# One core, attention + FFN + 2-D FFT + FFN: two groups of rows moved behind the second weight matrix, squares to a free tile, a third staging tile for part of the first matrix

## The chip, the core and the metric

One NeuronCore of one Trainium2 chip runs the whole program in one launch. The metric is device time in microseconds (us) of one execution, and the time of a kernel is the median of its runs.

## What is computed

Inputs are q, k, v of 4 batches x 8 heads x 576 positions x 64, two feed-forward networks (FFNs) and a layer-norm gain; everything is float32.

```python
# attention, block-causal with blocks of 64
scores = scale * q @ k.T
scores = where(i // 64 >= j // 64, scores, -1e9)
attn   = softmax(scores) @ v                 # heads side by side: x is 4 x 576 x 512
# FFN 1
xn = (x - mean) / sqrt(var + 1e-6) * g_ln
x  = x + relu(xn @ w_ch1) @ w_ch2            # 512 -> 2048 -> 512
# FFT mixing and FFN 2
u  = x + real(fft(fft(x, axis=1), axis=2))
un = (u - mean) / sqrt(var + 1e-6)
out = u + relu(un @ w2_ch1) @ w2_ch2
```

## The kernel before

TensorE works in f16 here. A float32 operand is split into a high and a low f16 half, and each product is the sum of three f16 matmuls (high x high, high x low, low x high).

**Rows.** The 576 rows of each batch are split in three. E is the first 256 rows, F the next 256, and the last 64 rows of all four batches together form L (256 rows). So there are nine column blocks for each FFN: E0 to E3, F0 to F3 and L. FFN 1 goes over them in the order E0 E1 E2 E3 F0 F1 L F2 F3.

**Attention for E** (`e_items`): 16 units, one for a batch and a pair of heads. A unit loads q, k and v, makes fp32 scores (TensorE, L716), takes maxima (VectorE, L730, L731), the exponential (ScalarE, L734), splits the result into halves (ScalarE L688, VectorE L689), has it transposed by a DMA that SP issues (L695), multiplies it with v (TensorE, `pv`, L664; v is split by L677) and normalises (VectorE, L702, L705, L768).

**Attention for F and L** (`attention_items`): 16 units of three steps. Scores are L876, and the results leave through L943 (into `N`) and by GpSimd's DMAs (L970) into `XxF` and `XxL`. These units need another set of buffers, which is opened by `a_switch`. That item needs the whole second weight matrix of FFN 1 (`("W", 1, 2, 3)`) and the last rows of E (`("X1", "E3")`).

**Weights of FFN 1.** The two matrices have four chunks (`c`) each, and each chunk comes in two pieces of 1 MB: 16 pieces. `piece(k)` first lets SP load piece k + PL, with PL = 1 (`w_load`, L179, into a tile of the tag `stage`, of which there are ST = 2). Then come `w_raw` (ScalarE, L191) and `w_decode`: ScalarE writes a shifted copy into the one tile `sign` (L204), VectorE puts the bits together (L208, L211), and after two operations of VectorE ScalarE squares the chunk so far (L221), to get the sum of squares for the scale. The squares themselves are not used, and they are written over the raw piece in the stage tile. When the two pieces of a chunk of the first matrix are decoded, `w_hi` (ScalarE, L288) and `w_lo` (VectorE, L296) write the two halves into a tile `wq`. Chunks of the second matrix wait for scales that take all of them into account, made by `w_balance` (L249 to L259) after the last piece.

**FFN 1.** `gemm1` (L515, 192 matmuls of 128x256 for a column block), relu and split (ScalarE L524, VectorE L525), then `gemm2` (L540, 96 matmuls of 128x512) or, for E0, E1 and F3, `gemm2_both` (L570); its output is added by L555. Ahead of it stands the layer norm (L433 to L482), whose result is transposed by a DMA on SP (L483). L's tiles are `bn1L`, `ln1L`, `xs` and `xnT1L`.

**Order.** No engine order is written out. The items above stand in streams; `merge` takes the next item from the stream with the smallest virtual time, if what the item needs has been issued. Every engine then works through its own instructions in that program order. Tiles of one tag go round in a pool (`w` has 9, each 16 KB a partition), and the first write to a tile waits for the last reader of what was there.

**After FFN 1's attention** `a_end` frees the attention's buffers, and `w_second` loads and decodes the weights of FFN 2 with the same functions (32 pieces of 512 KB, two staging tiles of the tag `wr`); then come the DFT's matmuls and FFN 2.

Of the kernel before, what the change touches and what calls it, by code (L numbers as in the profile page):

```python
# [10 lines left out]
I32 = mybir.dt.int32  # L11
BF16 = mybir.dt.bfloat16
# [23 lines left out]
LNP = ()  # L36
NZ = (1, 2)
PL = 1
S_W0 = 0.0
E1B = (3, 2, 2)  # L40
NB = 1
# [20 lines left out]
S_E2 = 50.0  # L62
# [21 lines left out]
def fused_kernel(ctx: ExitStack, tc: tile.TileContext, io: dict):  # L84
# [4 lines left out]
    wpool = ctx.enter_context(tc.tile_pool(name="wpool", bufs=1))  # L89
# [61 lines left out]
    def all_sum(src, n, name):  # L151
        r = sm.tile([128, n], F32, tag="ar", name=name)
        nc.gpsimd.partition_all_reduce(r, src, 128, bass_isa.ReduceOp.add)
        return r


    W = {}
    wst = {"n": 0, "loaded": []}

    def w_stage(n, name):  # L160
        shape = [128, n, 512, 2]
        if "pool" in wst:
            return wst["pool"].tile(shape, I32, tag="wr", bufs=WR, name=name)
        return a_tile(shape, I32, "stage", name)

    def w_signs(pool, n, bufs):
# [29 lines left out]
    def w_decode(ffn, which, c, i, n):  # L196

        r = W.pop(("raw", ffn, which, c, i))
        dst = W["st", ffn, which, c][:, i:i + n, :]
        di = dst.bitcast(I32)  # L200
        hw, lw = r[:, :, :, 1], r[:, :, :, 0]
        z = wst["z"][wst["n"] % len(wst["z"])]
        wst["n"] += 1
        nc.scalar.activation(  # L204
            out=z[:, :, :, 1], in_=hw.bitcast(F32), func=AF.Copy, scale=float(2.0 ** -100)
        )
        zi = z.rearrange("p n f w -> p n (f w)").bitcast(I32)
        nc.vector.scalar_tensor_tensor(  # L208
            out=di, in0=di, scalar=3, in1=zi, op0=ALU.logical_shift_left, op1=ALU.bitwise_or
        )  # L210
        nc.vector.scalar_tensor_tensor(  # L211
            out=di, in0=lw, scalar=29, in1=di, op0=ALU.logical_shift_right, op1=ALU.bitwise_or
        )
        m = SQ[ffn - 1]
        if i == 0:
            W["n2", ffn, which, c] = sm.tile([128, 4 // m], F32, tag="wn", bufs=3, name="wn")
        if (i + n) % m:
            return
        rb = r.rearrange("p n f w -> p (n f w)").bitcast(BF16)
        k = i + n - m  # L220
        nc.scalar.activation(  # L221
            out=rb[:, 0:512 * m].rearrange("p (n f) -> p n f", n=m),
            in_=W["st", ffn, which, c][:, k:k + m, :], func=AF.Square,
            accum_out=W["n2", ffn, which, c][:, k // m:k // m + 1],
        )

    def w_total(ffn, which, c):

        n2 = W.pop(("n2", ffn, which, c))
        if n2.shape[-1] > 1:  # L230
            n1 = sm.tile([128, 1], F32, tag="wn1", bufs=2, name="wn1")
            nc.vector.tensor_reduce(out=n1, in_=n2, axis=AX.X, op=ALU.add)
            n2 = n1
        W["tot", ffn, which, c] = all_sum(n2, 1, "wt")
        if which == 1:
            W["t", ffn, which, c] = w_tile(ffn, which, c)

    def w_scale(ffn, which, c):
# [33 lines left out]
    def w_tile(ffn, which, c):  # L272
        if ffn == 2 and which == 1:
            return wst["pool"].tile([128, 2, 2048], F16, tag="w", bufs=2, name=f"wq{ffn}{which}{c}")
        return wpool.tile([128, 2, 2048], F16, tag="w", bufs=9, name=f"wq{ffn}{which}{c}")
# [92 lines left out]
    def w_items():  # L368

        n = WN[0]  # L370
        pieces = [(which, c, i) for which in (1, 2) for c in range(4) for i in range(0, 4, n)]

        def load(k):
            if k < len(pieces):
                w_load(1, *pieces[k], n)

        todo = []

        def piece(k):
            which, c, i = pieces[k]  # L380
            load(k + PL)
            w_raw(1, which, c, i, n)
            w_decode(1, which, c, i, n)
            scales()
            if i + n == 4:
                w_total(1, which, c)
                todo.append((which, c))

        def scales():

            for which, c in todo:
                w_scale(1, which, c)
                if which == 1:
                    w_hi(1, which, c)
                    w_lo(1, which, c)
            todo.clear()

        def end(c):
            if c == 0:
                scales()  # L400
                w_balance(1)
            w_hi(1, 2, c)
            w_lo(1, 2, c)

        first = [(0.0, lambda k=k: load(k), (), None) for k in range(PL)]
        out = ([], [])
        for k, (which, c, i) in enumerate(pieces):
            gives = ("W", 1, 1, c - 1) if which == 1 and i == 0 and c > 0 else None
            out[which - 1].append((float(n), lambda k=k: piece(k), (), gives))
        out[0].append((0.0, scales, (), ("W", 1, 1, 3)))  # L410
        for c in range(4):
            out[1].append((1.0, lambda c=c: end(c), (), ("W", 1, 2, c)))
        return first, out[0], out[1]
# [190 lines left out]
    def a_tile(shape, dt, tag, name):  # L604
        return ap_["p"].tile(shape, dt, tag=tag, bufs=ap_["b"][tag], name=name)
# [167 lines left out]
    def e_items(b):  # L773
        def head():
            e_raw(b, 0)
            e_load(b)

        def front(p):
            if p + 1 < NPAIR:
                e_raw(b, p + 1)  # L780
            e_s(b, p)
            e_exp(b, p)
            e_norm_p(b, p)

        def back(p):
            e_pv(b, p)
            e_x(b, p)

        out = [(0.0, head, (), None), (3.0, lambda: front(0), (), None), (1.0, lambda: e_v(b), (), None)]
        for p in range(1, NPAIR):  # L790
            out.append((3.0, lambda p=p: (front(p), back(p - EL) if p >= EL else None), (), None))
        for p in range(NPAIR - EL, NPAIR):
            out.append((1.0, lambda p=p: back(p), (), ("X1", ("E", b)) if p == NPAIR - 1 else None))
        return out
# [440 lines left out]
    if True:  # L1235
# [31 lines left out]
        a_open(dict(stage=ST, rv=RVE, raw=RAWE, vh=2, vl=2, e=E1B[0], P=E1B[1], PT=E1B[2], xnT0=1, xn0=X0B, xs0=X0B))  # L1267
        w_signs(ap_["p"], WN[0], NZ[0])
        AE = [e_items(b) for b in range(B)]
        A1 = [(0.0, a_switch, (("W", 1, 2, 3), ("X1", ("E", 3))), None)]  # L1270
        A1 += attention_items([(b, p) for b in range(B) for p in range(NPAIR)])
        A1 += [(0.0, a_end, (), ("X1", "L"))]

# [67 lines left out]
        for c in range(4):  # L1341
# [6 lines left out]
            (0.0, 1.0, LN),  # L1348
            (0.0, 1.0, AE[0]),
            (S_E1, 1.0, AE[1]),  # L1350
            (S_E2, 1.0, AE[2] + AE[3]),
            (S_W0, 1.0, WF),
            (S_W1, R_W, WA),
            (S_W2, R_W, [(0.0, lambda: None, (("W", 1, 1, 3),), None)] + WB1),
            (S_F, 1.0, FF),
            (S_A1, R_A1, A1),
            (S_D, R_D, D),
# [104 lines left out]
```

## Time and profile before

| | |
|---|---|
| median of 3 runs | 1038.68 us (1035.98 to 1040.9) |
| the profiled execution | 1037.72 us, of which the span in the trace is 1035.9 us |
| busy: TensorE (PE) | 941.0 us, 91% of the span |
| busy: VectorE (DVE), ScalarE (ACT), GpSimd (POOL) | 617.5, 501.7, 83.9 us |
| mean granted TensorE clock | 0.959 of full speed (full speed is 2.4 GHz, the other level 1.2 GHz) |

A row of a timeline gives the start in us from the span's start, the duration in us, the engine, the line and operation, out<-in and a count; square brackets tell how long the engine was idle before and what released it. SPq is the DMA queue that SP issues on, and its rows are the time of issuing, not of moving.

### The profile page before, as it was taken

Reading aid. Unit: us, or ns where it says so; the run is one execution under the profiler, and the core shown is the slowest. Engines: PE = TensorE matmul, PEld = TensorE weight load, DVE = VectorE, ACT = ScalarE, POOL = GpSimd, SP = SyncE. Lnnn points to the kernel's source line nnn. Section 1 sums busy time; section 2 is a strip of 40 time slices with the busy share of each in tenths; the row PEclk is TensorE's granted clock in tenths of the full one; section 3 lists DMA queues with packets and bytes.
Section 4 is the critical chain, followed back from the end, with each engine's and each line's share of the span. In section 5 each row is a group of like instructions: output and inputs, shape, how many; then the busy total and the mean of one; then the engine's idle time right before and its main releaser. Section 6 shows DMA issues by size and latency. Waiting matters only on the chain.

```text
span 1035.9 us, 18326 instructions
## 1 busy us (share of the span) xinstructions
PE 941.0 (91%) x7226; PEld 645.6 (62%) x7226; DVE 617.5 (60%) x1501; ACT 501.7 (48%) x884; POOL 83.9 (8%) x217
## 2 busy tenths in 40 slices
PE   5467859889899989999998979999999999999998
PEld 4355644467476566576574756767668577586673
DVE  5879788777777876675477979865332332222120
ACT  6678775667677677535466765632111021120110
POOL 2101001000202002031011111100000000000000
PEclk9578978999999999999999989999999999999999
DMA  7876865456767758446415275630110100200100
GB/s 204 227 169 187 228 155 111 92 117 139 152 147 135 148 118 161 86 117 174 102 41 148 86 222 194 218 87 12 31 31 11 41 21 22 31 22 31 31 11 21
DMA packets 172439, 110.84 MB, mean 107 GB/s; under 512 B 146893, under 2 KB 155094, under 8 KB 170816
## 3 DMA queue, kind: packets, MB, share of 16 engines
q1 hardware_dynamic: 170032, 105.41, 41.4%
q0 software_dynamic: 2320, 4.25, 1.8%
q8 instruction: 57, 0.93, 0.4%
q14 instruction: 30, 0.25, 0.1%
HBM read 59.95 MB, written 11.01 MB: 68 GB/s over the span
## 4 chain that ended last, share of the span: by engine, by line
PE 45%; DVE 5%; DMA 4%; ACT 2%; issue 1%; POOL 0%; ACTq 0%; DVEq 0%
PE g L515 20%; PE g L540 19%; PE g L570 4%; DMA wr<-in_w 3%; DMA xnT1L<-xs 1%; PE ya L1143 1%; ACT wr L221 1%; DVE ws L211 1%; PE pq L1174 1%; DVE ws L208 1%; DVE hT L525 1%; ACT sign L204 1%; DVE wq L296 1%; PE pq L1164 1%; PE pf L1164 1%
## 5 line engine op out<-in xcount | busy, mean ns | idle before, releaser
L515 PEld LDWEIGHTS <-wq 128*128 128x128 f16 x3456 | 338.0, 99 | 66.9 <-ACT wq L288 6.2
L540 PE MATMUL g<-wq,hT 128*128 128x512 f16 x1440 | 331.2, 379 | 0.6 <-DVE XxE L555 0.6
L540 PEld LDWEIGHTS <-hT 128*128 128x128 f16 x1440 | 139.9, 98 | 161.1 <-issue 4.4
L524 ACT ACTIVATE hT<-g 128x512 f16<-128x512 f32 x144 | 84.5, 590 | 241.5 <-PE g L515 241.4
L525 DVE SCALAR_TENSOR_TENSOR hT<-g,hT 128x512 f16<-128x512 f32 x144 | 98.6, 687 | 140.6 <-ACT hT L524 140.4
L664 PE MATMUL pv<-vh,PT 128*128 128x65 f16 (+1 forms) x800 | 106.8, 206 | 32.9 <-DMA PT<-P 26.6
L664 PEld LDWEIGHTS <-PT 128*128 128x128 f16 x1200 | 85.0, 102 | 61.0 <-DMA PT<-P 29.4
L876 PE MATMUL st<-k,qz 128*128 128x512 f16 (+2 forms) x288 | 80.9, 334 | 13.8 <-ACT e L898 13.8
L689 DVE SCALAR_TENSOR_TENSOR P<-e,P 128x768 f16<-128x768 f32 (+2 forms) x64 | 62.0, 971 | 40.3 <-ACT P L688 39.9
L898 ACT ACTIVATE e<-st,aq,acf 128x384 f32<-128x384 f32 (+2 forms) x80 | 56.8, 740 | 53.7 <-DVE aq L893 48.9
L664 PE MATMUL pv<-vl,PT 128*128 128x64 f16 (+1 forms) x400 | 66.9, 205 | 3.0 <-DVE vl L677 3.0
L570 PE MATMUL g<-wq,hT 128*128 128x512 f16 x288 | 66.2, 388 | 0.7 <-DVE wq L296 0.7
L191 ACT ACTIVATE ws<-wr 128x512 f32<-128x512 f32 (+1 forms) x48 | 39.5, 827 | 43.4 <-DMA wr<-in_w 40.9
L688 ACT ACTIVATE P<-e 128x768 f16<-128x768 f32 (+2 forms) x64 | 54.4, 858 | 3.8 <-DMA PT<-P 2.3
L208 DVE SCALAR_TENSOR_TENSOR ws<-ws,sign 128x512 int32<-128x512 int32 (+1 forms) x48 | 41.5, 866 | 19.7 <-ACT sign L204 18.0
L716 PE MATMUL st<-raw 128*128 128x128 f32 (+1 forms) x128 | 39.5, 449 | 15.1 <-ACT e L734 7.6
L482 DVE TENSOR_TENSOR xs<-xn,xs 128x512 f16<-128x512 f32 x36 | 24.6, 687 | 45.4 <-ACT xs L476 45.4
L570 PEld LDWEIGHTS <-hT 128*128 128x128 f16 x288 | 28.7, 100 | 35.6 <-issue 3.8
L476 ACT ACTIVATE xs<-xn 128x512 f16<-128x512 f32 x36 | 22.4, 625 | 57.9 <-DMA xnT2('E', 3)_10326<-xs 7.8
L204 ACT ACTIVATE sign<-wr 128x512 f16<-128x512 f32 (+1 forms) x48 | 46.5, 968 | 5.7 <-DMA wr<-in_w 4.3
L892 DVE TENSOR_REDUCE aq<-st 128x2 f32<-128x768 f32 (+2 forms) x48 | 46.6, 972 | 2.5 <-PE st L684 1.7
L221 ACT ACTIVATE wr<-ws 128x512 bf16<-128x512 f32 (+1 forms) x40 | 35.3, 882 | 25.8 <-DVE ws L211 22.7
(385 smaller groups left out, 1298.8 us busy)
## 6 DMA issues: line engine op xcount, KB each, us to landing
wr<-in_w SPq DMA_DIRECT2D x16, 1024.0 KB, 5.9
wr<-in_w SPq DMA_DIRECT2D x32, 512.0 KB, 4.1
rawv<-in_vt SPq DMA_DIRECT2D x16, 320.0 KB, 3.8
rawqk<-in_kt SPq DMA_DIRECT2D x16, 288.0 KB, 2.9
out<-out SPq DMA_DIRECT2D x18, 256.0 KB, 2.0
d<-ws SPq DMA_DIRECT2D x4, 1024.0 KB, 5.0
ws<-d SPq DMA_DIRECT2D x4, 1024.0 KB, 7.9
rawqk<-in_qt SPq DMA_DIRECT2D x32, 80.0 KB, 3.4
```

Of the source, the lines that this page charges most:

```text
L204: nc.scalar.activation(out=z[:, :, :, 1], in_=hw.bitcast(F32), func=AF.Copy, scale=float(2.0 ** -100))
L208: nc.vector.scalar_tensor_tensor(out=di, in0=di, scalar=3, in1=zi, op0=ALU.logical_shift_left, op1=ALU.bitwise_or)
L515: nc.tensor.matmul(out=ps[:, i, :], lhsT=w1(ffn, k, wh, m), rhs=xt[:, xh, k, :], start=(n == 0), stop=(n == 3 * KT - 1),)
L524: nc.scalar.activation(out=h[:, :, 0, :], in_=ps, func=AF.Relu)
L525: nc.vector.scalar_tensor_tensor(out=h[:, :, 1, :], in0=ps, scalar=0.0, in1=h[:, :, 0, :], op0=ALU.max, op1=ALU.subtract,)
L540: nc.tensor.matmul(out=ps, lhsT=h[f // 4][:, f % 4, hh, t * 128:(t + 1) * 128], rhs=w2(ffn, f, wh), start=(f == 0 and hh == 0 and wh == 0) ...
L570: nc.tensor.matmul(out=g2["b"][t], lhsT=h[f // 4][:, f % 4, hh, t * 128:(t + 1) * 128], rhs=w2(ffn, f, wh), start=(f == 0 and hh == 0 and ...
L664: nc.tensor.matmul(out=out[..., 0:w], lhsT=l, rhs=v[..., 0:w], start=(n == 0), stop=(n == len(mm) - 1))
L688: nc.scalar.activation(out=P[:, 0, 0:n], in_=e, func=AF.Copy, scale=PSC)
L689: nc.vector.scalar_tensor_tensor(out=P[:, 1, 0:n], in0=e, scalar=PSC, in1=P[:, 0, 0:n], op0=ALU.mult, op1=ALU.subtract)
L876: nc.tensor.matmul(out=st[:, h, 0:n] if j < 4 else sf[:, o:o + n], lhsT=qz[:, a, q:q + 128], rhs=k[:, c, o:o + n], start=(i == 0), stop=(j ...
L898: nc.scalar.activation(out=e[:, h], in_=st[:, h], func=AF.Exp, scale=cf, bias=nb[:, h:h + 1],)
```

## The change

Line numbers of the changed kernel are higher than those of before by 4 (loads, L179 is L183), 15 (FFN and attention, L515 is L530, L876 is L891) and so on.

1. The stream of E2 and E3's attention gets an empty first item that needs chunk 0 of the second matrix to be issued in its final form. E2 and E3 therefore follow that chunk in program order, where they ran beside the weights before.
2. The squares of FFN 1's weights go into a tile of the tag `w`: for the first matrix into the tile that receives `wq` afterwards, for the second matrix into one tile for all chunks. The stage tile has its last reader at the second operation of VectorE (L211, now L215) instead of the square. FFN 2's squares stay in place.
3. Pieces 2, 5 and 8 are staged in a tile of the tag `w` in place of a stage tile, and up to piece 10 the load runs two pieces ahead, behind that one.

```diff
--- before.py
+++ after.py
@@ -36,6 +36,7 @@
 LNP = ()
 NZ = (1, 2)
 PL = 1
+T3 = 10
 S_W0 = 0.0
 E1B = (3, 2, 2)
 NB = 1
@@ -161,6 +162,9 @@
         shape = [128, n, 512, 2]
         if "pool" in wst:
             return wst["pool"].tile(shape, I32, tag="wr", bufs=WR, name=name)
+        wst["k"] = wst.get("k", -1) + 1
+        if wst["k"] % 3 == 2 and wst["k"] < T3:
+            return wpool.tile(shape, I32, tag="w", bufs=9, name=name)
         return a_tile(shape, I32, "stage", name)
 
     def w_signs(pool, n, bufs):
@@ -216,8 +220,16 @@
             W["n2", ffn, which, c] = sm.tile([128, 4 // m], F32, tag="wn", bufs=3, name="wn")
         if (i + n) % m:
             return
-        rb = r.rearrange("p n f w -> p (n f w)").bitcast(BF16)
         k = i + n - m
+        if ffn == 1:
+
+            if which == 1 or c == 0:
+                W["sq"] = w_tile(1, which, c)
+            if which == 1:
+                W["t", 1, which, c] = W["sq"]
+            rb = W["sq"][:, 0, :].bitcast(BF16)
+        else:
+            rb = r.rearrange("p n f w -> p (n f w)").bitcast(BF16)
         nc.scalar.activation(
             out=rb[:, 0:512 * m].rearrange("p (n f) -> p n f", n=m),
             in_=W["st", ffn, which, c][:, k:k + m, :], func=AF.Square,
@@ -232,7 +244,7 @@
             nc.vector.tensor_reduce(out=n1, in_=n2, axis=AX.X, op=ALU.add)
             n2 = n1
         W["tot", ffn, which, c] = all_sum(n2, 1, "wt")
-        if which == 1:
+        if (ffn, which) == (2, 1):
             W["t", ffn, which, c] = w_tile(ffn, which, c)
 
     def w_scale(ffn, which, c):
@@ -375,10 +387,13 @@
                 w_load(1, *pieces[k], n)
 
         todo = []
+        state = {"next": PL}
 
         def piece(k):
             which, c, i = pieces[k]
-            load(k + PL)
+            while state["next"] <= (k + 2 if k + 2 <= T3 else k + 1):
+                load(state["next"])
+                state["next"] += 1
             w_raw(1, which, c, i, n)
             w_decode(1, which, c, i, n)
             scales()
@@ -1267,6 +1282,7 @@
         a_open(dict(stage=ST, rv=RVE, raw=RAWE, vh=2, vl=2, e=E1B[0], P=E1B[1], PT=E1B[2], xnT0=1, xn0=X0B, xs0=X0B))
         w_signs(ap_["p"], WN[0], NZ[0])
         AE = [e_items(b) for b in range(B)]
+        AE2 = [(0.0, lambda: None, (("W", 1, 2, 0),), None)] + AE[2]
         A1 = [(0.0, a_switch, (("W", 1, 2, 3), ("X1", ("E", 3))), None)]
         A1 += attention_items([(b, p) for b in range(B) for p in range(NPAIR)])
         A1 += [(0.0, a_end, (), ("X1", "L"))]
@@ -1348,7 +1364,7 @@
             (0.0, 1.0, LN),
             (0.0, 1.0, AE[0]),
             (S_E1, 1.0, AE[1]),
-            (S_E2, 1.0, AE[2] + AE[3]),
+            (S_E2, 1.0, AE2 + AE[3]),
             (S_W0, 1.0, WF),
             (S_W1, R_W, WA),
             (S_W2, R_W, [(0.0, lambda: None, (("W", 1, 1, 3),), None)] + WB1),
```

**TensorE at the first score of F and L** (`st<-k`, from line L876 to L891). `g` is an FFN's PSUM output; `hT` is the activation of FFN 1. Before:

```order
L570 LDWEIGHTS hT
L570 MATMUL g_1690<-wq_1766,hT 128x512
L876 LDWEIGHTS qz_1798
L876 MATMUL st<-k_1837,qz_1798 128x384
L570 LDWEIGHTS hT
```

Now:

```order
L530 LDWEIGHTS wq_378
L530 MATMUL g_2077<-xnT1('E', 2)_1995,wq_378 128x256
L891 LDWEIGHTS qz_1910
L891 MATMUL st<-k_1938,qz_1910 128x384
L530 LDWEIGHTS wq_378
```

Before, 384 matmuls of `gemm1` (E0 and E1) and 91 matmuls of `gemm2_both` stand ahead of the first score; now all 192 of `gemm2_both` for E0 and E1 stand ahead of it, and 4 of E2's `gemm1` too, while 10 of the 16 units of E, not 16, are transposed ahead of the last load of weights. At the other end, 30 matmuls of `gemm1` and 96 of `gemm2` stand between the last `pv` and L's first matmul before, and 32 of `gemm2` now.

**VectorE at the end of the attention** (`rr` is the reciprocal that follows a `pv`, `bn1L` the first step of L's layer norm). Before:

```order
L943 TENSOR_TENSOR N_5101<-pv,rr 128x128
L525 SCALAR_TENSOR_TENSOR hT<-g_5705,hT 128x2x256
L525 SCALAR_TENSOR_TENSOR hT<-g_5762,hT 128x2x256
L433 BN_STATS bn1L_6032<-XxL 128x6
L434 BN_AGGR ln1L<-bn1L_6032 128x2
L433 BN_STATS bn1L_6035<-XxL 128x6
L433 BN_STATS bn1('F', 2)0_6419<-XxF_5224 128x6
L434 BN_AGGR ln1L<-bn1L_6035 128x2
L525 SCALAR_TENSOR_TENSOR hT<-g_5789,hT 128x2x256
L702 TENSOR_SCALAR rr<-pv,pw 128x2
```

Now:

```order
L717 TENSOR_SCALAR rr<-pv,pw 128x2
L720 RECIPROCAL rr<-rr 128x2
L448 BN_STATS bn1L_6033<-XxL 128x6
L449 BN_AGGR ln1L<-bn1L_6033 128x2
L448 BN_STATS bn1L_6036<-XxL 128x6
L448 BN_STATS bn1('F', 2)0_6471<-XxF_5403 128x6
L449 BN_AGGR ln1L<-bn1L_6036 128x2
L449 BN_AGGR ln1('F', 2)_6470<-bn1('F', 2)0_6471 128x2
L451 TENSOR_SCALAR ln1L<-ln1L 128x2
L448 BN_STATS bn1('F', 2)1_6474<-XxF_5403 128x6
L454 TENSOR_SCALAR ln1L<-ln1L 128x2
L570 SCALAR_TENSOR_TENSOR XxF_4446<-g_5893,winv_1266,XxF_4446 128x512
```

L's layer norm stood ahead of the last `rr` (the last rows of before), and now it stands behind it; an output of `gemm2` of F1 (L570, which was L555) now stands inside its chain.

**SP at the same place** (`wr_...<-in_w_2` are the first loads of FFN 2's weights). Before:

```order
L695 DMA_TRANSPOSE PT<-P 128x16x128
L695 DMA_TRANSPOSE PT<-P 128x10x128
L483 DMA_TRANSPOSE xnT1L<-xs 128x8x128
L179 DMA wr_6293<-in_w_2 128x1024
L179 DMA wr_6342<-in_w_2 128x1024
L483 DMA_TRANSPOSE xnT1L<-xs 128x8x128
```

Now:

```order
L710 DMA_TRANSPOSE PT<-P 128x16x128
L710 DMA_TRANSPOSE PT<-P 128x10x128
L183 DMA wr_6156<-in_w_2 128x1024
L183 DMA wr_6193<-in_w_2 128x1024
L498 DMA_TRANSPOSE xnT1L<-xs 128x8x128
L183 DMA wr_6255<-in_w_2 128x1024
L183 DMA wr_6289<-in_w_2 128x1024
L498 DMA_TRANSPOSE xnT1L<-xs 128x8x128
```

Two loads of FFN 2's weights moved ahead of the first transpose of L's rows, and two more ahead of the second.

## Rows read from the trace of the kernel before

**Rows 1.** The page: span, and DMA issues (KB each, us to landing).
```profile
span 1035.9 us, 18326 instructions
...
wr<-in_w SPq DMA_DIRECT2D x16, 1024.0 KB, 5.9
```

**Rows 2.** Windows: length, then PE, PEld, DVE, ACT, POOL busy, clock, DMA share, GB/s.
```profile
25.00:157.00 132.00, 87.00 (x759) 71.22 (x757) 108.09 (x268) 99.58 (x151) 12.04 (x33) 0.76 0.78 194
...
188.00:458.00 270.00, 249.07 (x2375) 170.31 (x2373) 200.60 (x521) 184.65 (x336) 28.14 (x74) 0.99 0.63 129
...
524.00:700.00 176.00, 166.16 (x1177) 117.03 (x1175) 148.56 (x370) 109.19 (x210) 22.78 (x59) 0.97 0.47 146
700.00:1036.00 336.00, 332.12 (x2292) 223.97 (x2289) 89.25 (x179) 46.61 (x78) 0.20 (x2) 1.00 0.09 24
```

**Rows 3.** ScalarE's groups, 0 to 260 us: busy, mean ns | idle before, releaser.
```profile
L204 ACT ACTIVATE sign<-wr 128x1024 f16<-128x1024 f32 x16 | 21.8, 1361 | 1.3 <-DVE ws L208 1.3
L191 ACT ACTIVATE ws<-wr 128x1024 f32<-128x1024 f32 x16 | 18.2, 1140 | 20.8 <-DMA wr<-in_w 20.8
...
L221 ACT ACTIVATE wr<-ws 128x2048 bf16<-128x2048 f32 x8 | 15.3, 1910 | 4.8 <-DVE ws L211 4.8
```

**Rows 4.** A wait of SP's queue, 0 to 260 us: us in total, times, longest.
```profile
SPq L179 <- ACT wr L221: 19.8, 4, 6.6
```

**Rows 5.** VectorE's groups, 0 to 260 us: busy, mean ns | idle before.
```profile
L689 DVE SCALAR_TENSOR_TENSOR P<-e,P 128x768 f16<-128x768 f32 x21 | 20.0, 952 | 6.4 <-ACT P L688 6.1
...
L730 DVE TENSOR_REDUCE eq<-st 128x2 f32<-128x512 f32 x16 | 10.9, 681 | 0.0
...
L768 DVE TENSOR_TENSOR XxE<-pv,rr 128x256 f32<-128x256 f32 x16 | 6.7, 420 | 0.0
L730 DVE TENSOR_REDUCE eq<-st 128x2 f32<-128x256 f32 x16 | 6.7, 419 | 9.4 <-PE st L684 9.4
...
L677 DVE SCALAR_TENSOR_TENSOR vl<-rv,pw,vh 128x1024 f16<-128x1024 f32 x4 | 5.1, 1280 | 1.4 <-ACT vh L676 1.4
...
L705 DVE RECIPROCAL rr<-rr 128x4 f32<-128x4 f32 x16 | 2.8, 173 | 0.1
```

**Rows 6.** Timelines at the balance: VectorE, then TensorE up to the first score.
```profile
156.92 0.22 DVE L259 TENSOR_SCALAR wsc<-wz,wzm 128x4 f32<-128x4 f32 x1
160.31 20.09 PE L570 MATMUL g<-wq,hT 128*128 128x512 f16 x89 [0.65 <-DVE wq L296]
180.24 0.33 PE L876 MATMUL st<-k,qz 128*128 128x384 f16 x1
```

**Rows 7.** TensorE's timeline: scores of a unit of E, and a start after idling.
```profile
81.60 1.11 PE L716 MATMUL st<-raw 128*128 128x256 f32 x4
...
88.81 8.04 PE L515 MATMUL g<-xnT,wq 128*128 128x256 f16 x50 [6.04 <-DVE ln1('E', 1)_787 L451]
```

**Rows 8.** TensorE's timeline from the last `pv` to L.
```profile
455.83 0.22 PE L664 MATMUL pv<-vh,PT 128*128 128x130 f16 x1
455.89 3.44 PE L515 MATMUL g<-xnT1('F', 1)_5363,wq 128*128 128x256 f16 x30
459.17 20.88 PE L540 MATMUL g<-wq,hT 128*128 128x512 f16 x96
479.89 13.30 PE L515 MATMUL g<-xnT1L,wq 128*128 128x256 f16 x120
```

**Rows 9.** L's layer norm: GpSimd's and VectorE's timelines, then the chain that ended last.
```profile
449.43 1.00 POOL L970 DMA_DIRECT2D XxL<-N  x2
451.40 0.69 DVE L433 BATCH_NORM_STATS2 bn1L<-XxL 128x6 f32<-128x512 f32 x1
458.22 2.29 DMA XxF<-N
464.08 10.03 DMA xnT1L<-xs
```

**Rows 10.** SP's timeline while the stage tiles are full.
```profile
24.36 7.30 SPq L695 DMA_TRANSPOSE PT<-P  x2
```

## The prediction

> **What bounds the kernel now.** I read the windows first, because the span is made of stages with different limits. From 700 us on, TensorE is busy for 332.1 of 336 us, and from 524 to 700 for 166.2 of 176 [rows 2]: behind L the end moves with TensorE's work, and only some 10 us of gaps can be won there. From 188 to 458 us it is busy for 249.1 of 270, so 21 us of gaps. From 25 to 157 us it is busy for 87 of 132, at a mean clock of 0.76, while VectorE is busy for 108.1 and ScalarE for 99.6 [rows 2]. This is the stage in which weights are decoded and E's attention runs, and neither engine is full: 23.9 us of VectorE's time there is idle, 18%.
>
> Next I asked what ends the idle time. ScalarE's first operation on a piece (L191) stood idle for 20.8 us, all of it for the weights' DMA [rows 3]. SP's own wait for a free stage tile is 19.8 us in four waits, put down to the square [rows 4]. So weights arrive late in part because a stage tile is held through VectorE's two operations and a 1.91 us square [rows 3].
>
> The timelines give the marks on which I build the sum: the balance of the second matrix's scales ends at B = 157 us, the first score of F and L stands at C = 180.2 [rows 6], the last `pv` at D = 455.9, and L's first matmul at E = 479.9 [rows 8]. From E on there is nothing but TensorE's work and its few gaps, so I ask how far E moves, then what the rest gives back.
>
> **B: the weights' stage.** Six of E's units move behind it. One unit costs VectorE 0.952 + 0.681 + 0.419 + 0.420 us and three small operations like the reciprocal's 0.173, together 3.0 us; six are 18.0. Two splits of v (1.28 each) go with them, 2.6, and about a dozen small operations of E2's layer norm at 0.17, 2.0 [rows 5]. VectorE thus loses 22.6 of 108.1 us, and 85.5 is left. What I can't read off is the idle time that remains. With the same idle share (18%) the stage takes 85.5/0.82 = 104 us and B' = 129; with the same 23.9 us idle B' = 134; with half of it, because the earlier release and the third tile remove the waits for a stage tile, B' = 122; with 16 of the 23.9 gone, 118. Speaking for a share that stays: the wait that goes is only part of the idle time, and the units that are left still make VectorE wait for TensorE and ScalarE (the 9.4 us ahead of L730, the 6.4 ahead of L689) [rows 5]. I take **B' = 130**, and keep 118 and 136 as ends.
>
> The squares cost as much as before, in another tile. For the first matrix that tile is the one that `w_hi` writes behind them on the same engine, so no new wait lies on it; if a tile of the tag still had a reader, the square would wait on ScalarE with that engine's next pieces queued behind it. In the program order no reader of such a tile stands late, and I price this at nothing, or 2 us.
>
> **C: the first score of F and L.** Before, this followed B by 23 us. The work that used to be ahead of B is now behind it, so it doesn't vanish: TensorE must do all 192 matmuls of `gemm2_both` for E0 and E1, at 20.09/89 = 0.226 us (interleaved starts included; 0.216 net, as 20.88/96 shows) [rows 6, 8]: 41.4 us. Add the 3.4 us from the balance to the second block's start [rows 6], 142 attention products of 65 columns, estimated from the 512-column row at 0.03 each, 4 us, scores of three units at about 1.7 (1.11 for the four wide ones, half of it for the narrow ones [rows 7]), 5 us, and 0.4 for four of E2's `gemm1`. That is 54; for waits on the last units' transposes I add 2. **C' = B' + 56 = 186**, 5.8 later than before. Less work on VectorE early and more TensorE work ahead of the attention nearly cancel here.
>
> **D: the last `pv`.** The FFN work ahead of C grew by 101 x 0.216 + 4 x 0.11 = 22.2 us. The work behind D shrank: before, 30 matmuls of `gemm1` and 96 of `gemm2`, 24.0 us from D to E [rows 8]; now 32 x 0.216 = 6.9. So 24.0 - 6.9 = 17.1 us more stands ahead of D in all, and between C and D there is 22.2 - 17.1 = 5.1 us less than in the 275.7 of before. D' = 186 + 275.7 - 5.1 = **456.6**, 0.7 later. This supposes that the attention's pace stays TensorE's, as 249 busy of 270 say [rows 2].
>
> **E: L's layer norm comes too late for its cover.** Before, `bn1L` began at 451.4, which is 4.5 us ahead of the last `pv`, and L's transposed rows landed at 464.08 + 10.03 = 474.1 [rows 9]: a chain of 22.7 us, inside the 24.0 of FFN work that ran over it. In the new order `bn1L` stands behind the last `rr`, and what it reads must go through the last evacuation of L, GpSimd's issue (1.00) and a landing like the 2.29 [rows 9]: 0.2 + 0.2 + 0.3 for VectorE, 3.3 for the copy and some 0.5 between them, 4.5 us behind the last `pv`. The chain itself I leave at 22.7: two FFN 2 loads moved ahead of each transpose, but the 10 us landing already has such loads beside it. Only 6.9 us of work covers 27.2, so TensorE stands for some 20 us. A start after a long idle costs extra: 50 matmuls took 8.04 us after 6 us of idling [rows 7], where 13.30/120 = 0.111 each [rows 8] makes 5.5, so 2.5. E' = D' + 4.5 + 22.7 + 2.5 = D' + 29.7 = **486.3**, 6.4 later. Bounds of the step: 24.0, if the layer norm gets ahead after all, and 33, if the loads hold up both transposes.
>
> **Behind E.** The program's decoding of FFN 2's weights stands about 5 us further ahead of L's matmuls than before, and 9.8 us of TensorE's time from 524 to 700 is idle [rows 2]; I take 3 us of gain from it (bounds 0 and 5).
>
> **Sum.** +5.8 (C) - 5.1 + 5.7 (E against D) - 3 = +3.4. On the profiled execution (1037.7 us: 1035.9 of span [rows 1] and 1.8 around it) that is 1041.1, and on the median of the runs, 1038.7, it is 1042.1. I say **1041.5**.
>
> **The rivals.** *The weights' waits vanish* (faster). If a piece is always there when ScalarE turns to it, B' is 118: C' = 174, D' = 444.6, E' = 474.3, and the end -5.6 - 3 = -8.6, so about 1029. For it speaks that 20.8 of L191's idle time is for the DMA alone [rows 3]; against it, that VectorE's and ScalarE's own alternation (the one `sign` tile: L204 waits for L208, L208 for L204) is unchanged. It decides as soon as B' is below 121.
>
> *More loads in SP's queue* (slower). A 1 MB load lands in 5.9 us [rows 1], and the queue's transposes can stand for a long time: issuing two took 7.30 us at 24.4 [rows 10]. If one of the three extra loads in flight goes in front of a transpose on the path, B' = 136, and if E's last units, which now share the queue with the attention's loads, come 3 us late as well, the end is +3.4 + 5.9 + 3 = +12.3: 1050. It decides from B' = 132 on. The Trainium skill ("DMA: Bandwidth & Descriptors", sections "Queues, rings and completion order" and "Issuing engines are not separate DMA queues") speaks for it: what SP issues shares one row of rings over the same 16 engines, and each ring is consumed in order, so a transpose behind a load waits for it; by that rule the end would be this rival's 1050, and without it the forecast's. The 7.30 us agrees with that, without showing which transfer was waited for.
>
> *The change does not cost at L* (E' = D' + 24, the layer norm covered as before because the last rows of L are ready early): +3.4 - 5.7 = -2.3, about 1036. For it: in time, `rr` of the last unit may come before L's rows have landed. Against: with 6.9 us of FFN work left there is little to cover even the old start.
>
> **Chances and range.** The forecast, a wash with ends at 1036 and 1046, 0.42; waits vanish 0.27; loads in the queue 0.15; no cost at L 0.16. A measurement of this kernel tells about 0.5%, 5.2 us, from no change. Of the forecast 0.25 is within that and 0.17 above it (only 1.8 us above my B' it goes past the bound); the last rival gives 0.11 within and 0.05 faster. Faster 0.27 + 0.05 = 0.32, same 0.36, slower 0.17 + 0.15 = 0.32. The range goes to B' = 118 with 5 us given back, 1027 (-10.6), and to 1054, the loads' case with an E step 4 us longer.
>
> **What would show it.** Right: the balance near 130 us, the first score near 186, the last `pv` near 457, and a gap of about 20 us on TensorE ahead of L's first matmul, ended by `xnT1L`, at a lower clock just behind it. Wrong: the balance below 121 or above 134, L191 no longer waiting for its DMA, transposes issued for 7 us and more around pieces 2, 5 and 8, or no gap ahead of L. What hurts most if I am mistaken is the idle share in the weights' stage, since every us of B' goes to the end.

## The result, and the profile after

The changed kernel takes 1048.19 us (median of 4 runs, 1043.95 to 1056.32), the kernel before 1037.33 beside it: the ratio is 1.0109, 95% interval 1.0074 to 1.0144, so 1.1% slower. Its own profile is of the longest of these executions (1056.3 us). I had the same kernel profiled a second time, in an execution of 1044.9 us, and read both. The second is 3.3 us below the median.

The marks in the first profile, VectorE's and then TensorE's timeline (the balance, the first score of F and L, the last `pv`, what covers L, and L):

```profile
134.61 0.22 DVE L271 TENSOR_SCALAR wsc<-wz,wzm 128x4 f32<-128x4 f32 x1
...
194.02 0.33 PE L891 MATMUL st<-k,qz 128*128 128x384 f16 x1
...
469.66 0.22 PE L679 MATMUL pv<-vh,PT 128*128 128x130 f16 x1
469.72 7.07 PE L555 MATMUL g<-wq,hT 128*128 128x512 f16 x32
492.62 7.64 PE L530 MATMUL g<-xnT1L,wq 128*128 128x256 f16 x46 [15.83 <-DMA xnT1L<-xs]
```

The same marks in the second:

```profile
133.09 0.22 DVE L271 TENSOR_SCALAR wsc<-wz,wzm 128x4 f32<-128x4 f32 x1
...
190.15 0.33 PE L891 MATMUL st<-k,qz 128*128 128x384 f16 x1
...
459.44 0.22 PE L679 MATMUL pv<-vh,PT 128*128 128x130 f16 x1
459.49 7.07 PE L555 MATMUL g<-wq,hT 128*128 128x512 f16 x32
482.59 7.58 PE L530 MATMUL g<-xnT1L,wq 128*128 128x256 f16 x51 [16.03 <-DMA xnT1L<-xs]
```

Both agree that the balance comes some 23 us earlier than before, that the first score comes 10 to 14 us later all the same, and that TensorE stands for 16 us ahead of L, where it did not stop before [rows 6, 8]. They differ between the first score and the last `pv`: 275.6 us in the one, 269.3 in the other.

Two windows of the first profile, from the balance to the first score and from there to the last `pv` (length, then PE, PEld, DVE, ACT, POOL busy, clock, DMA share, GB/s):

```profile
134.60:194.00 59.40, 55.99 (x382) 29.66 (x381) 44.30 (x111) 28.93 (x54) 5.97 (x15) 0.93 0.46 91
194.00:469.70 275.70, 252.36 (x2382) 171.86 (x2381) 201.49 (x501) 187.68 (x341) 25.62 (x70) 0.98 0.65 127
```

The windows of the second profile, cut at its marks, with the same columns:

```profile
25.00:133.10 108.10, 73.29 (x596) 59.23 (x597) 91.45 (x211) 88.64 (x124) 9.56 (x28) 0.82 0.76 203
...
0.00:133.10 133.10, 85.86 (x680) 69.04 (x681) 103.26 (x246) 102.40 (x149) 16.12 (x49) 0.84 0.76 204
133.10:190.20 57.10, 53.58 (x383) 28.66 (x382) 44.49 (x111) 28.93 (x54) 5.97 (x15) 0.99 0.48 93
190.20:459.50 269.30, 248.82 (x2383) 170.26 (x2381) 201.25 (x501) 187.59 (x341) 26.09 (x70) 0.99 0.66 131
459.50:482.60 23.10, 7.07 (x36) 3.03 (x33) 15.86 (x62) 8.13 (x16) 11.48 (x22) 0.71 0.72 195
482.60:705.00 222.40, 208.90 (x1449) 144.16 (x1450) 168.19 (x401) 126.02 (x245) 23.78 (x55) 0.96 0.45 137
```

The first row is the weights' stage alone; in the five behind it, length less PE busy gives TensorE's idle time: 47.2, 3.5, 20.5, 16.0 and 13.5 us. The fourth of these is new; in the kernel before no such window exists, since TensorE worked from the last `pv` to L without a stop. Against the first profile, this one is 8.7 us shorter from the balance to the last `pv`, and 6.0 of that is TensorE's busy time: 302.4 us in place of 308.4 for as many matmuls (2766 and 2764), at a granted clock of 0.99 in both windows in place of 0.93 and 0.98.

One of ScalarE's groups from 0 to 157 us of the first profile, and then a wait of SP's queue up to 150 us:

```profile
L195 ACT ACTIVATE ws<-wr 128x1024 f32<-128x1024 f32 x16 | 17.7, 1135 | 3.5 <-DMA wr<-in_w 3.5
```

```profile
SPq L183 <- DVE ws L215: 20.5, 4, 8.0
```

The wait for the weights' DMA, 20.8 us before [rows 3], is 3.5. SP still waits 20.5 us for staging tiles, on VectorE's second operation in place of the square (19.8 us before [rows 4]), but the loads are now early enough that ScalarE hardly waits for them.

Around L, in the second profile, the chain that ended last and then the timelines of GpSimd and SP:

```profile
460.93 3.00 DMA XxL<-N
463.95 0.71 DVE bn1L L448
```

```profile
460.93 1.00 POOL L985 DMA_DIRECT2D XxL<-N  x2
...
465.01 0.81 SPq L183 DMA_DIRECT2D wr<-in_w  x2
472.75 1.23 SPq L498 DMA_TRANSPOSE xnT1L<-xs  x1
474.17 2.12 SPq L183 DMA_DIRECT2D wr<-in_w  x2
477.44 1.23 SPq L498 DMA_TRANSPOSE xnT1L<-xs  x1
```

What SP's queue waited for ahead of the first of these loads:

```profile
SPq L183 <- DMA XxL<-N: 9.9, 1, 9.9
```

The layer norm starts 4.5 us behind the last `pv` and L's first matmul follows 18.6 us after that. Before, the chain had 22.7 us, because its last transpose took 10.03 us to land [rows 9]; here it has landed 5.1 us after it was issued. In the 4 us behind L's first matmul the granted clock is 0.50 and then 0.55, near the lower of its two levels (1.2 GHz), and 1.00 from 486.6 us on; ahead of it TensorE had stood for 16 us.

### The profile page after: what moved, and what is told of

Same layout as the page of the kernel before. It is cut to its first block, busy times and chain, and to the rows that moved or that the text cites. A ratio compares the mean times of both kernels' runs of the same rounds, so it can differ in the third digit from the quotient of the medians.

```text
span 1054.5 us, 18349 instructions
## 1 busy us (share of the span) xinstructions
PE 947.8 (90%) x7226; PEld 645.9 (61%) x7226; DVE 624.3 (59%) x1501; ACT 501.0 (48%) x884; POOL 83.7 (8%) x217
## 4 chain that ended last, share of the span: by engine, by line
PE 40%; DVE 5%; DMA 5%; ACT 4%; issue 3%; POOL 1%; POOLq 0%; ACTq 0%; DVEq 0%
PE g L530 18%; PE g L555 16%; DMA wr<-in_w 5%; PE g L585 4%; ACT sign L208 1%; DVE ws L215 1%; ACT wr L233 1%; PE ya L1158 1%; DVE ws L212 1%; ACT wq L300 1%; PE pq L1189 0%; DVE hT L540 0%; ACT ws L195 0%; PE pf L1179 0%; DMA PT<-P 0%
## 5 line engine op out<-in xcount | busy, mean ns | idle before, releaser
L530 PEld LDWEIGHTS <-wq 128*128 128x128 f16 x3456 | 338.9, 99 | 93.0 <-DMA xnT1L<-xs 16.3
L555 PE MATMUL g<-wq,hT 128*128 128x512 f16 x1440 | 335.2, 381 | 0.6 <-DVE hT L540 0.6
L555 PEld LDWEIGHTS <-hT 128*128 128x128 f16 x1440 | 140.1, 98 | 154.9 <-issue 1.5
L679 PE MATMUL pv<-vh,PT 128*128 128x65 f16 (+1 forms) x800 | 103.7, 204 | 24.2 <-DMA PT<-P 23.2
L891 PE MATMUL st<-k,qz 128*128 128x512 f16 (+2 forms) x288 | 84.3, 337 | 9.5 <-ACT e L913 9.5
L704 DVE SCALAR_TENSOR_TENSOR P<-e,P 128x768 f16<-128x768 f32 (+2 forms) x64 | 62.0, 971 | 32.8 <-ACT P L703 32.5
L585 PE MATMUL g<-wq,hT 128*128 128x512 f16 x288 | 67.3, 392 | 0.0
L491 ACT ACTIVATE xs<-xn 128x512 f16<-128x512 f32 x36 | 22.4, 625 | 57.2 <-DVE xn L483 13.6
L215 DVE SCALAR_TENSOR_TENSOR ws<-wr,ws 128x512 int32<-128x512 int32 (+1 forms) x48 | 41.2, 864 | 0.4
```

The source lines that it names most:

```text
L530: nc.tensor.matmul(out=ps[:, i, :], lhsT=w1(ffn, k, wh, m), rhs=xt[:, xh, k, :], start=(n == 0), stop=(n == 3 * KT - 1),)
L555: nc.tensor.matmul(out=ps, lhsT=h[f // 4][:, f % 4, hh, t * 128:(t + 1) * 128], rhs=w2(ffn, f, wh), start=(f == 0 and hh == 0 and wh == 0) ...
L585: nc.tensor.matmul(out=g2["b"][t], lhsT=h[f // 4][:, f % 4, hh, t * 128:(t + 1) * 128], rhs=w2(ffn, f, wh), start=(f == 0 and hh == 0 and ...
L679: nc.tensor.matmul(out=out[..., 0:w], lhsT=l, rhs=v[..., 0:w], start=(n == 0), stop=(n == len(mm) - 1))
L704: nc.vector.scalar_tensor_tensor(out=P[:, 1, 0:n], in0=e, scalar=PSC, in1=P[:, 0, 0:n], op0=ALU.mult, op1=ALU.subtract)
L891: nc.tensor.matmul(out=st[:, h, 0:n] if j < 4 else sf[:, o:o + n], lhsT=qz[:, a, q:q + 128], rhs=k[:, c, o:o + n], start=(i == 0), stop=(j ...
```

## Experiments

Each was timed in rounds beside the kernel before; "ratio" is to that kernel, with its 95% interval.

**1. The change again** (nothing edited).

> The changed kernel once more, nothing edited, because its one profile is of an execution of 1056.3 us, 8 us above the median of its runs (1048.2). If the excess is chance, this profile shows the balance again near 134 us, the first score near 194 and TensorE idle for some 16 us ahead of L's first matmul, and the difference to 1056 lies between the first score and the last pv or behind L. If the kernel itself has two ways to run, its runs fall into two groups some 8 us apart.

1050.22 us, ratio 1.0117 (1.0081 to 1.0153). The marks repeat, and the difference to the first profile lies mostly between the balance and the last `pv` (8.7 of 11.4 us). All eight executions spread over 1044.0 to 1056.3 without two clear groups, so the excess of the first profile is scatter of this kernel, more than half of it TensorE's own work at a lower granted clock.

**2 and 3. The two parts apart.** The move alone, on the kernel before:

```diff
+        AE2 = [(0.0, lambda: None, (("W", 1, 2, 0),), None)] + AE[2]
...
-            (S_E2, 1.0, AE[2] + AE[3]),
+            (S_E2, 1.0, AE2 + AE[3]),
```

> Only the move of E2 and E3 behind the second matrix; squares in place and two stage tiles as before. Theory 1 (the move costs: it takes the cover off L's layer norm and puts the chain of six units of E between the balance and the first score; the staging gains): slower than the whole change, the balance at 138 to 148, first score at 198 to 205, the same gap of some 16 us ahead of L, 1053 to 1060. Rival (the staging itself costs, through more loads in SP's queue): faster than the whole change, balance at 130 or below, about 1040.

The staging alone is the changed kernel with those three lines undone.

> Only the staging: squares to a free tile and every third piece of the first matrix in a tile of the weights' tag, up to two pieces ahead; E2 and E3 where they were before. Theory 1: ScalarE's wait for the weights' DMA falls from 20.8 to about 4 us and the balance comes 6 to 15 us earlier (142 to 151), the first score as much, L is covered as before: 1024 to 1032. Rival A (VectorE's and ScalarE's own alternation sets the pace): the wait for the DMA goes but others take its place, balance at 153 to 157, 1035 to 1039. Rival B (more loads in SP's queue hold up transposes): balance after 157, 1040 or more.

The move alone: 1065.15 us, ratio 1.026 (1.0225 to 1.0294). The staging alone: 1030.26 us, ratio 0.9933 (0.9911 to 0.9955). So the move loses more than the whole change does, and the staging gains. In the move alone, the timelines of VectorE at the balance and of SP at the last load of FFN 1's weights, then the waits of ScalarE and SP up to 150 us, then the window from 25 us to the balance:

```profile
154.68 0.23 DVE L259 TENSOR_SCALAR wsc<-wz,wzm 128x4 f32<-128x4 f32 x1
140.16 0.37 SPq L179 DMA_DIRECT2D wr<-in_w  x1
```

```profile
ACT ws L191 <- DMA wr<-in_w: 19.0, 9, 5.9
SPq L179 <- ACT wr L221: 28.0, 5, 9.0
```

```profile
25.00:154.70 129.70, 82.44 (x636) 67.49 (x637) 97.21 (x225) 94.28 (x142) 11.51 (x32) 0.75 0.67 177
```

These are the rows to learn from. Six units of E were moved, and the balance came 2 us earlier (157 to 154.7), well short of the theory's 138 to 148; the time, 1065, is 5 us beyond the theory's 1060. The scores of all 16 units still ran ahead of the balance (64 wide score matmuls, as before), and VectorE's work in the stage fell by 10.9 us (108.1 [rows 2] to 97.2), not by the 22.6 of the prediction. Most of that became idle time: 32.5 us, where it was 23.9. With two stage tiles the weights' own round trip (load, decode, release, load) sets the pace; SP's wait for a tile at the square grew from 19.8 us [rows 4] to 28.0, ScalarE's for the weights stayed (20.8 before [rows 3], 19.0 now), and the room that the units left stayed empty. The rest of their work then comes behind the balance, and the first score follows at 205.9, not 180.2. The gap ahead of L is here too (15.85 us). In the staging alone, inside the theory's ranges, the balance is at 144.0 and the first score at 169.7, with E2 and E3 still beside the weights.

**4. Cover for L by another order of FFN 1's blocks.**

```diff
-ORDER1 = "E0 E1 E2 E3 F0 F1 L F2 F3"
+ORDER1 = "E0 E1 E2 E3 F0 F1 F2 L F3"
```

> The changed kernel with FFN 1's blocks in the order F0 F1 F2 L F3, so that 101 matmuls of gemm2 and 192 of gemm1 (43 us) stand between the last pv and L's first matmul. Theory 1 (the gap ahead of L is a loss of its own): the gap of 16 us goes, with the slow start behind it, and the end comes 10 to 18 us earlier than the whole change's, about 1032 to 1038. Rival (the gap only shows time that is lost anyway, since the DFT and FFN 2 wait for L and the decoding of FFN 2's weights sets their start): the gap goes, but TensorE idles as long in the DFT; within 4 us of the whole change.

1044.31 us, ratio 1.007 (1.0046 to 1.0094). It falls at the edge of the rival's expectation, 3.9 us under the first median of the change and 5.9 under the second, and far from theory 1's 1032 to 1038. Windows from the last `pv` on:

```profile
469.20:513.00 43.80, 43.06 (x296) 28.69 (x295) 28.93 (x66) 24.96 (x49) 9.91 (x19) 1.00 0.54 171
513.00:705.00 192.00, 170.58 (x1169) 119.20 (x1168) 140.39 (x341) 108.23 (x208) 21.72 (x51) 0.93 0.42 138
```

The gap is gone, but from L to 705 us TensorE now idles for 21.4 us, against 13.5 in the changed kernel. With L 30 us later, the DFT, which waits for L, has less FFN 1 work beside it; that this is the reason was not tested. The last `pv`, too, is 9.7 us later than in the second profile of the change; 27 more matmuls of `gemm2` (5.8 us) stand ahead of it in this order. So this run can't tell whether the gap is the loss, since it opens others.

**5. Cover for L by the pace, the order of blocks as it was.**

```diff
-R_A1 = 0.8
+R_A1 = 0.70
```

> The changed kernel with the attention of F and L let further ahead of the FFN in program order (R_A1 from 0.8 to 0.70), so that between the last pv and L's first matmul stand 30 matmuls of gemm1 and 96 of gemm2, exactly as in the kernel before the change. Theory 1 (the loss of the move is the gap on TensorE ahead of L, 16 us and 2.5 us of slow start; up to L the move saves TensorE about 5 us of idling): gap gone, 12 to 19 us faster than the whole change, 1028 to 1037, and no slower than the staging alone by more than 6 us. Rival (the gap is only where lost time shows; with FFN work kept back the attention lacks it, and TensorE idles between the first score and the last pv in place of it): TensorE idle there rises from 21 to 30 us and more, 1041 to 1048.

1033.26 us, ratio 0.9954 (0.9934 to 0.9974), 1.5% faster than the change itself and inside theory 1's 1028 to 1037. TensorE's timeline behind the last `pv`:

```profile
445.12 0.22 PE L679 MATMUL pv<-vh,PT 128*128 128x130 f16 x1
445.18 3.44 PE L530 MATMUL g<-xnT1('F', 1)_5320,wq 128*128 128x256 f16 x30
448.45 20.88 PE L555 MATMUL g<-wq,hT 128*128 128x512 f16 x96
469.17 6.06 PE L530 MATMUL g<-xnT1L,wq 128*128 128x256 f16 x54
```

The same 30 and 96 matmuls as before the change [rows 8] run into L with no stop. The rival asked for 30 us of idling between the first score and the last `pv`; that window says 22.4:

```profile
186.00:445.20 259.20, 236.76 (x2304) 163.13 (x2303) 200.47 (x506) 188.64 (x343) 28.79 (x73) 0.99 0.71 137
445.20:469.20 24.00, 24.00 (x129) 12.31 (x128) 15.89 (x61) 7.56 (x15) 10.17 (x19) 1.00 0.79 154
```

So the attention did not lack the work that was held back for L, and closing the gap brings back 15 us, more than the whole change had lost. It does not follow that the move costs nothing else: runs 9 to 11.

**6. Half of the move**: E3 alone waits, E2 runs beside the weights.

```diff
-        AE2 = [(0.0, lambda: None, (("W", 1, 2, 0),), None)] + AE[2]
...
-            (S_E2, 1.0, AE2 + AE[3]),
+            (S_E2, 1.0, AE[2] + [(0.0, lambda: None, (("W", 1, 2, 0),), None)] + AE[3]),
```

> The changed kernel, with E3 alone behind the second matrix and E2 beside the weights as before; 77 matmuls of gemm2 (16.6 us) stand between the last pv and L. Theory 1: TensorE idles ahead of L for about 7 us in place of 16, balance at 138 to 141, 1034 to 1041, between the staging alone and the whole change. Rival (the chain of units behind the balance costs, by the unit): three units there in place of six, the first score near 180, and still 1038 to 1044.

1034.06 us, ratio 0.997 (0.9945 to 0.9995), at the lower end of theory 1's range, with the balance at 139.6 and the first score at 175.4. TensorE at the end of the attention:

```profile
451.77 16.78 PE L555 MATMUL g<-wq,hT 128*128 128x512 f16 x77
470.43 2.78 PE L530 MATMUL g<-xnT1L,wq 128*128 128x256 f16 x24 [1.87 <-DMA xnT1L<-xs]
```

16.8 us of cover leaves 1.9 us of idling, less than the 7 expected: the layer norm started 0.05 us behind the last `pv` here (at 451.76), in place of 4.5.

**7 and 8. The staging in two parts**, without the move. Squares in a free tile alone, from the staging (`T3 = 1` leaves no piece to a third tile and loads one piece ahead):

```diff
-T3 = 10
+T3 = 1
```

> Only the squares to a free tile; two stage tiles, loads one piece ahead, no move. The earlier release of a stage tile is worth about the square's 1.9 us and what stands ahead of it on ScalarE, eight times. Theory 1 (the release is most of the staging's gain): balance at 146 to 150, 1030 to 1034. Rival (the third tile is most of it): balance at 152 to 156, 1034 to 1038.

The third tile alone, squares in place:

```diff
-        if ffn == 1:
...
-            if which == 1 or c == 0:
-                W["sq"] = w_tile(1, which, c)
...
-            rb = W["sq"][:, 0, :].bitcast(BF16)
-        else:
-            rb = r.rearrange("p n f w -> p (n f w)").bitcast(BF16)
+        rb = r.rearrange("p n f w -> p (n f w)").bitcast(BF16)
...
-        if (ffn, which) == (2, 1):
+        if which == 1:
```

> Only pieces 2, 5 and 8 in a tile of the weights' tag, with loads up to two pieces ahead; squares in place, no move. Theory 1 (the release is most of the gain): balance at 150 to 155, 1033 to 1037. Rival (the third tile is most of it): balance at 146 to 149, 1029 to 1033, and the wait for the weights' DMA is as small as with both.

Squares alone: 1037.6 us, ratio 1.0011 (0.9992 to 1.003), no change, with the balance at 152.0. The third tile alone: 1028.13 us, ratio 0.9923 (0.9898 to 0.9948), balance at 144.9. The rival of both was right, and the third tile came out a little better than it said: without the move, the third tile is the gain. A wait of SP's for a staging tile before, up to 150 us, which comes on top of [rows 4]; then, up to 152 us, SP's and ScalarE's waits with the squares alone and SP's with the third tile alone:

```profile
SPq L179 <- DVE ws L211: 6.2, 2, 3.3
```

```profile
SPq L183 <- DVE ws L215: 26.7, 8, 6.1
ACT ws L195 <- DMA wr<-in_w: 7.6, 4, 2.7
```

```profile
SPq L183 <- DVE ws L215: 2.2, 2, 1.4
SPq L183 <- ACT wr L225: 1.2, 2, 0.9
```

Before, SP waited 19.8 us for the square and 6.2 for VectorE's second operation, 26.0 together. Released ahead of the square, the tile is waited for as long (26.7), and the name of the releaser changed. Another tile takes the wait away (3.4). The release had an effect all the same: ScalarE's wait for the weights fell from 20.8 us [rows 3] to 7.6 and the balance came 5 us earlier, but the time did not change. From the balance to the first score it took 25.7 us, where it took 23.3 before, and from there to the last `pv` 279.9 us, where it took 275.7; of the latter difference 3.5 us are TensorE's busy time for the same 2393 matmuls, at a granted clock of 0.98 in place of 0.99.

**9 to 11. The move with cover, on each staging, and a control.** All have `R_A1 = 0.70`: the move alone, the move with the third tile, and the third tile without the move.

> The move alone (squares in place, two stage tiles), with R_A1 = 0.70, so that L has the cover it had before the change. Theory 2 (with two stage tiles the weights' loads set when the balance comes, so taking six units off that stage makes room that nothing uses, and their work comes on top behind it): balance still at 153 to 156, and 1044 to 1054, clearly slower than the kernel before although L is covered. Rival (the gap ahead of L was all that the move cost): 1033 to 1040.

> The third tile and the move, squares in place, R_A1 = 0.70. Theory 2 (with the loads early enough the move is about neutral once L is covered): 1026 to 1033, within 4 us of the third tile alone. Rival (the move would gain, if nothing else stood against it): 1018 to 1025.

> A control: the third tile alone, no move, R_A1 = 0.70, so that L has 34 us of cover in place of 24. If the pace itself were a gain, this would be faster than the third tile alone (1028) by several us, and the gain of the paced change would not be L's cover; by theory 1 a cover of 24 us is enough, and it is the same within 3 us, 1026 to 1031, or slower if the attention now lacks FFN work.

The move alone, covered: 1052.92 us, ratio 1.0128 (1.0078 to 1.0179), balance at 154.8, first score at 203.8. With the third tile: 1038.55 us, ratio 1.0003 (0.9981 to 1.0026), balance at 140.9, first score at 189.4. In both, the 30 and 96 matmuls run into L with no stop. So L's cover is not all that the move costs. Where the weights' loads set the balance, the move costs 1.3% even with L covered (against the kernel before, which was not run at this pace). With the third tile it costs 0.5% against the control at the same pace, 0.8% against the third tile alone. Where the squares leave the stage tiles too (run 5 against run 3), 0.2%, inside the intervals, is left. In this order the balance comes earlier, 154.8, 140.9 and 131.3 us; that the loss shrinks because of it is a reading of three points. None of them shows a gain from the move. The second theory held for the move alone; its 1026 to 1033 for the third tile with the move was missed by more than 5 us.

Run 10 differs from run 5 by the squares alone. With the move and the third tile, squares in a free tile bring the balance 9.6 us earlier and the time from 1.0003 to 0.9954, beyond the intervals; without the move they gave nothing (run 7, and run 3 against run 8).

The control, 1033.72 us, ratio 0.9956 (0.9931 to 0.9981), is not faster than the third tile alone (0.9923, 0.9898 to 0.9948), so the pace is no gain by itself. The expectation had its cover wrong: 48.6 us of FFN work stood behind the last `pv`, not 34.

**12. The third tile for piece 11 too** (`T3 = 13`).

> The third tile alone, for piece 11 as well (T3 = 13), so that loads run two pieces ahead into the second matrix. If waits for weights still set the pace in the second half, the balance comes 2 to 5 us earlier than with the third tile as it is (140 to 143) and 1023 to 1027; if the engines' own work sets it by then, the same, 1027 to 1029.

1032.13 us, ratio 0.994 (0.9914 to 0.9967), balance at 143.6. The time lies above both expectations, with the balance 1.3 us earlier than in run 8; it does not differ from the third tile as it is by more than the intervals allow. The lowest ratio is that of the third tile alone, with the squares in place and nothing moved: 0.9923 of the kernel before. It is not clear of the staging alone (0.9933).

## Why the prediction was right, and where it was not

The range held the time, but the sum said +3.4 us and the medians differ by about +11. At 1048.2 us the kernel lies past the 1046 that the forecast gave as its own upper end; it lies inside the range because that reaches up to 1054 for the rival of the loads, which the runs do not bear out. That part is luck. The prediction was right for the mechanism that the sum names for L, and wrong in some sizes and in the sign of its last term. The second profile has a span 7.2 us over that of before: +9.9 up to the first score, -6.3 from there to the last `pv`, +1.0 up to L with the slow start behind it, and +2.6 from there on. The prediction had +5.8, -5.1, +5.7 and -3, so the errors of the last two (-4.7 and +5.6) nearly cancel. By its steps:

- **B.** 130 forecast, 133.1 and 134.6 measured. VectorE was left with more work than I had counted (91.5 us from 25 us to the balance, against 85.5), because scores of units that I took as moved still ran there (50 of the 64 wide score matmuls of E ran ahead of the balance, 12.5 units' worth and not 10), and it idled for 15%, where I took 18. The two partly cancel. But the reason was incomplete: "VectorE thus loses 22.6" moves the balance only because the staging is there. Run 2 made the same move with two tiles; VectorE lost 10.9 us, and the balance moved by 2.
- **The squares.** I read SP's 19.8 us as weights that arrive late since a stage tile is held through a square. Run 7 bears this out in part: ScalarE's wait for the weights fell to 7.6 us without the third tile, but SP's wait passed to VectorE's operation ahead of the square, and the time did not change.
- **C.** C' = B' + 56 was 57.1 and 59.4: 1 and 3 us short. C itself is 4 and 8 us later than forecast, mostly by B.
- **D.** 5.1 us less between C and D was 6.3 less in one profile and none in the other, where the granted clock was lower.
- **E.** The cover of 6.9 us is 7.07, the idle time forecast as some 20 is 16.0, and the start of the layer norm 4.5 us behind the last `pv` is exact. From D to E it took 23.1 us, and 1.9 more of slow start follows (51 matmuls in 7.58 us, at 0.111 each 5.7), against 29.7 forecast. The chain was mis-sized by 4 us: I left the transpose at its 10.03 us, taking FFN 2's loads beside it for the reason, and it landed in 5.1 with such loads just ahead of it. The lower clock behind the gap, forecast too, was there (0.50).
- **Behind E.** This step failed in sign. I took 3 us of gain from the earlier decoding of FFN 2's weights. Behind E the second profile has 560.5 us, before 556.0. In program order the loads are further ahead; in time they are not. They were issued 5.5 us behind the last `pv` before (461.3 against 455.8) and 5.6 us behind it now (465.0 against 459.4), where SP's queue had stood for 9.9 us until L's rows left the attention. The order showed a place and I read a time from it. Of the 4.5 us, 1.9 are the slow start and 2.0 are TensorE's idle time from E to 705 us, 13.5 against 11.5 in as long a stretch of before.

The rivals: the weights' waits did vanish (20.8 to 3.5), but the balance did not go to 118, because VectorE is by then busy for 85% of the stage. The rival of the loads was to decide from B' = 132 on, and the balance came at 133 to 135. But its other sign, a transpose issued for 7 us around pieces 2, 5 and 8, is absent: up to 90 us none takes longer than 3.5 us in the changed kernel, and the 7.30 us of before [rows 10] is gone. More loads in SP's queue were not the loss either: the third tile, with the same loads in flight, made the kernel 0.8% faster. The Trainium skill ("DMA: Bandwidth & Descriptors", "Queues, rings and completion order") has what SP issues consumed in the order of its rings. L's transposes agree: in the second profile the one behind two loads landed after 5.1 us, the one with none just ahead after 2.8. The third rival is refuted by the 16 us gap.

What stays open: why the granted clock differs between executions of one kernel, which is over half of the one difference that two profiles show; why the balance 5 us earlier in run 7 gave nothing at the end, beyond the place where it was lost; and why the squares' tile helps only with the move.

## What to carry to other kernels

Work that runs in the idle time of a stage with another bound can cost next to nothing there (10.9 us of VectorE's work taken out in run 2 brought the stage's end 2 us earlier); before moving it out, ask whether the stage ends earlier without it, and take the answer from what paces the stage (here the round trip of two buffers), not from the busiest engine. When work is moved ahead in a stream, count what is left as cover for the next serial chain, here a layer norm with its transposes; a pace that restored the same 24 us of matmuls brought back 15 us. The order of instructions tells where something stands, not when it runs; look for what it waits for. A releaser named by a wait is the last of several: freeing a buffer ahead of it can hand the same wait to the one before, and another buffer is the test.

## What the runs showed of the hardware

The second transpose of L's rows landed 10.03 us after its issue before [rows 9] and 5.1 us after it in the changed kernel, though two of FFN 2's loads go out just ahead of it in both. What differs is GpSimd's queue. It issued the DFT's seven constants (1.2 MB) around that transpose's issue at 464.1 us before, and ahead of the one at 477.4 us in the changed kernel; the first and the last of them, before and then in the second profile of the change:

```profile
462.70 0.57 POOL L1035 DMA_DIRECT2D c_ct<-in_c_ct  x1
466.66 0.53 POOL L1039 DMA_DIRECT2D c_row<-in_c_row  x1
...
466.92 0.57 POOL L1050 DMA_DIRECT2D c_ct<-in_c_ct  x1
470.89 0.54 POOL L1054 DMA_DIRECT2D c_row<-in_c_row  x1
```

The other traces agree. In nine of the 14, one of L's two transposes was issued while the constants went out or up to 0.3 us ahead of them: it took 6.9 to 10.5 us to land, and the other of the pair 2.7 to 3.6. In run 5 it is the first that took 9.6 us, and L's first matmul waited for neither. In the five where neither was issued so close to the constants (the change twice, and runs 2, 4 and 11), the two took 2.8 to 6.0. This is a regularity over 14 traces; no run moved the constants alone.

Executions of one unchanged kernel spread by 12 us (1044 to 1056). Between its two profiles 8.7 of the 11.4 us lie between the balance and the last `pv`, and 6.0 of these are TensorE's busy time for as many matmuls at a lower granted clock; over the whole program the clock was 0.954 in the slower, 0.962 in the faster.
